# Layer 1's rectifier as one ScalarE function, a 128-row sinks' product, and port ties by deadline, in an attention and two-layer kernel

## The chip, the cores and the metric

One core of one Trainium2 chip runs the whole program. The time is device microseconds (us) of one execution, lower is better. TensorE is called PE, its weight loads PEld, VectorE DVE, ScalarE ACT, GpSimd POOL, SyncE SP.

## The reference, cut to what matters

Attention over a window of 128 keys and the first 4 keys of the sequence (the sinks), then two feed-forward layers without a residual:

```python
B, H, S, D = 2, 8, 768, 64            # n_sink = 4, window = 128
scores = (q @ k.T) / sqrt(D);  keep = (key < 4) or (0 <= query - key < 128)
x = softmax(where(keep, scores, -1e9)) @ v        # -> (1536, 512)
h1 = x @ w1_in;  x = maximum(0.01 * h1, h1) @ w1_out      # d_ff = 2048
h2 = x @ w2_in;  y = (h2 * sigmoid(h2)) @ w2_out
```

## The kernel before, in words

**Tiles.** A unit is one group of 256 queries of one batch and one pair of heads; there are 24, in the order of the groups, and each has two slots of 128 queries. Within a batch the groups are g = 0, 1, 2; the 16 units with g > 0 see the sinks apart from their window. A slot's work: `scores` (PE products `sc`, a DVE reduction that masks them into the tile `P` and keeps the largest in `sm`, the exponential on ACT), `normalise` (a reciprocal in `sm`, and a product by it on ACT for the first 16 slots, on DVE after), `transposes` (PE turns `P` into `tr`, ACT copies that to `pT`). `values` then multiplies `pT` by the values `v` into `at`.

**The sinks.** In a unit with g > 0 the 4 sink columns of both heads go to 24 columns of a tile `psink` in three forms: rounded (hi), the rest (lo), and hi once more. Three small GpSimd operations per slot make them (`normalise`, L619 to L621). PE transposes `psink` into columns of `at`, ACT copies two 32-row strips of it to `sink_t`, and one product `at<-sink_t,sk` of 64 rows (K = 64) and 256 columns begins the sum in `at` (`values`, L660). `sk` holds the sinks' values, made by two DVE operations (`sh`, `sk`) from a loaded tile `sr` (`load_v`).

**The layers.** 16 weight chunks of 128 hidden units per layer. A chunk comes as two halves of raw words (`wr`) and is converted by `load_half`: ACT, four DVE operations on `wb`, ACT and DVE into hi and lo halves of the tile `w` or `we`. Six chunks of layer 1 work beside the attention on tiles of 256 tokens (36 items, `item_h` and `item_y`); after the attention 30 items of layer 1 and 48 of layer 2 work on tiles of 512 tokens. An item is 12 products `h` and 12 products `ya` or `y`, each value as hi and lo parts. Between them `emit_h` makes `ga` (or `gb`), hi and lo, of `h`. In layer 1 that is four steps, of which each waits for the one before: ACT writes 0.01 h to `g`, DVE takes the larger of `g` and `h`, ACT rounds that into hi, DVE subtracts into lo:

```python
R.scalar.activation(g, hp, AF.Copy, scale=0.01)                                    # L474
R.vector.tensor_tensor(g, g, hp, op=ALU.max if layer == 0 else ALU.mult)           # L477
R.scalar.activation(gt[:, 0, :], g, AF.Copy)                                       # L478
R.vector.tensor_tensor(gt[:, 1, :], g, f32(gt[:, 0, :]), op=ALU.subtract)          # L479
```

**What sets the order.** Nothing is issued as it is written. A recorder collects the operations; `deadlines` walks back from TensorE's order to a due time for each; `order` then plays the program with a table of costs and picks, again and again, on each engine the operation that can start first (of equals, the one due first), and of the engines' candidates the one that starts first. A flag `port` marks GpSimd's operations and DVE's with two operands in SBUF (or one in and one out): the plan runs only one of those at a time. The order so found is each engine's queue; the engines then only wait on semaphores. As all instructions are issued from one place, every row of the profile has line L375, and groups go by tiles.

Of the kernel before, what the change touches and what calls it, by code (L numbers as in the profile page):

```python
# [8 lines left out]
F32 = mybir.dt.float32  # L9
F32R = mybir.dt.float32r  # L10
U32 = mybir.dt.uint32
BF16 = mybir.dt.bfloat16
AF = mybir.ActivationFunctionType
ALU = mybir.AluOpType
PSUM = bass.MemoryType.PSUM

P = 128
QB = 128
GT = 256
# [94 lines left out]
class Recorder:  # L114
# [148 lines left out]
    def order(self):  # L263

        for op in self.ops:
            op.need, op.est = len(op.deps), 0.0
            for d in op.deps:
                d.users.append(op)
        self.deadlines()
        free = dict.fromkeys(self.ENGINES, 0.0)  # L270
        dma = port = 0.0
        ready = {e: [o for o in self.ops if o.eng == e and not o.need] for e in self.ENGINES}
        nxt = {(p, t): 0 for p in self.pools for t in p.tiles}
        stages = {}
        for p in self.pools:
            if p.stage is not None:
                stages.setdefault(p.stage, []).append(p)
        n_left = {s: sum(len(ts) for p in ps for ts in p.tiles.values()) for s, ps in stages.items()}
        ended = dict.fromkeys(stages, 0.0)
        done = []  # L280

        def opening(op):

            at = 0.0
            for k, t in enumerate(op.opens):
                p = t.pool
                if nxt[p, t.tag] + sum(o.tag == t.tag for o in op.opens[:k]) != t.place:
                    return None
                if p.stage is not None and p.stage > 0:
                    if n_left[p.stage - 1]:  # L290
                        return None
                    at = max(at, ended[p.stage - 1] + 200)
                k = t.place - p.bufs[t.tag]
                if k >= 0:
                    old = p.tiles[t.tag][k]
                    if old.left:
                        return None
                    at = max(at, old.end + 150)
            return at

        while len(done) < len(self.ops):
            best = None
            for e in self.ENGINES:
                can = []
                for o in ready[e]:
                    at = max(o.est, free[e], port if o.port else 0.0)
                    if o.opens:
                        room = opening(o)
                        if room is None:
                            continue  # L310
                        at = max(at, room)
                    can.append((at, o.due, o.rank, o))
                if not can:
                    continue
                first = min(c[0] for c in can)
                start, _, _, o = min((c for c in can if c[0] <= first), key=lambda c: c[1:3])
                if best is None or start < best[0]:
                    best = (start, o)
            start, op = best
            op.start = start  # L320
            if op.bytes:
                free[op.eng] = start + (500 if op.eng == "sync" else 100)
                dma = max(dma, start + 1200) + max(op.bytes / 350.0, 370)
                end = dma + 300
            else:
                end = free[op.eng] = start + op.cost
                if op.port:
                    port = end
            op.end = end
            ready[op.eng].remove(op)  # L330
            done.append(op)
            for t in op.opens:
                nxt[t.pool, t.tag] += 1
            for t in op.tiles:
                t.left -= 1
                t.end = max(t.end, end)
                if not t.left and t.pool.stage is not None:
                    n_left[t.pool.stage] -= 1
                    ended[t.pool.stage] = max(ended[t.pool.stage], end)
            for u in op.users:  # L340
                u.est = max(u.est, (op.start if not u.deps[op] else end + self.lag(op, u)))
                u.need -= 1
                if not u.need:
                    ready[u.eng].append(u)
        return done
# [44 lines left out]
def attention_moe(ctx, tc, cfg, ins, out):  # L390
    R = Recorder(tc)
    B, H, S, D = cfg["shape"]
    n_sink, window, near = cfg["n_sink"], cfg["window"], cfg["near"]
    qkd, vd, w1, w2 = (ins[n] for n in ("qkd", "vd", "w1", "w2"))
    scale = 1.0 / float(np.sqrt(D))
    NP = H // 2
# [7 lines left out]
    attn = R.pool("attn", 0)  # L404
# [57 lines left out]
    def emit_h(gt, t, layer, T, t0, n):  # L462
        hp = ps.tile([P, 512], F32, "h", 2)[:, :n]
        last = KC * 3 - 1
        i = 0
        with R.group():
            for kc in range(KC):
                for a, b in ((0, xh), (1, xh), (0, xl)):
                    R.tensor.matmul(hp, wi(t, a, kc), b[T][:, kc, t0:t0 + n], start=i == 0, stop=i == last)
                    i += 1  # L470
        R.at_h = R.ops[-1]
        g = keep.tile([P, 512], F32, "g", 2)[:, :n]
        if layer == 0:
            R.scalar.activation(g, hp, AF.Copy, scale=0.01)  # L474
        else:
            R.scalar.activation(g, hp, AF.Sigmoid)
        R.vector.tensor_tensor(g, g, hp, op=ALU.max if layer == 0 else ALU.mult)  # L477
        R.scalar.activation(gt[:, 0, :], g, AF.Copy)  # L478
        R.vector.tensor_tensor(gt[:, 1, :], g, f32(gt[:, 0, :]), op=ALU.subtract)  # L479

    def emit_y(yps, gt, t, layer, c, first, last):
# [8 lines left out]
    if near:  # L490
        mask = [attn.tile([P, 260], BF16, f"mask{i}") for i in range(4)]
        psink = [attn.tile([P, P], F32, f"psink{i}") for i in range(2)]
        sink_t = [attn.tile([64, GT], F32R, f"sink_t{i}") for i in range(2)]

        qk_raw = [attn.tile([P, 2, GT + 388], F32, "qk" if i < 2 else "qkh", 2) for i in range(4)]

# [35 lines left out]
    state, sinks = {}, {}  # L532
# [26 lines left out]
    def load_v(n):  # L559
        if n >= len(units):  # L560
            return
        d = state[n]
        nb = d["nb"]
        d["v"] = attn.tile([P, 3, P], F32, "v", 3)
        R.sync.dma_start(out=d["v"][:, :nb], in_=vd[n][:, :nb])
        key = d["G"] // NG, d["p"]
        if d["g"] > 0 and key not in sinks:
            sr = attn.tile([64, P + 1], F32, "sr", 2)
            R.sync.dma_start(out=sr, in_=ins["vs"][key])

            sh = attn.tile([64, P], F32R, "sh", 1)
            R.vector.tensor_copy(sh, sr[:, :P])
            sinks[key] = attn.tile([64, P], F32R, "sk", NP + 1)
            R.vector.scalar_tensor_tensor(sinks[key], in0=f32(sh), scalar=sr[:, P:P + 1], in1=sr[:, :P],
                                          op0=ALU.mult, op1=ALU.add)

# [26 lines left out]
    def normalise(s):  # L603
        d = slots[s]
        pt, sm, n, i = d["pt"], d["sm"], d["n"], d["i"]
        R.bias = SOONER
        R.vector.tensor_scalar(sm[:, 2:4], sm[:, 2:4], 1.0e-9, None, op0=ALU.add)
        R.vector.reciprocal(sm[:, 2:4], sm[:, 2:4])
        for j in range(2):
            if s < ON_ACT:  # L610
                R.scalar.activation(pt[:, j, :n], pt[:, j, :n], AF.Copy, scale=sm[:, 2 + j:3 + j])
            else:
                R.vector.tensor_scalar(pt[:, j, :n], pt[:, j, :n], sm[:, 2 + j:3 + j], None, op0=ALU.mult)
        if d["g"] > 0:
            s0 = 2 * P if i == 0 else P
            src = pt[:, :, s0:s0 + NS]
            hi, lo, hi2 = (psink[s // 2 % 2][:, o:o + 2 * NS].rearrange("p (j s) -> p j s", j=2)
                           for o in range(32 * i, 32 * i + 6 * NS, 2 * NS))
            R.gpsimd.tensor_copy(hi.bitcast(F32R), src)  # L619
            R.gpsimd.tensor_tensor(lo.bitcast(F32R), src, hi, op=ALU.subtract)  # L620
            R.gpsimd.tensor_copy(hi2, hi)  # L621
        R.bias = 0

    def transposes(s):
# [136 lines left out]
    if near:  # L761
# [7 lines left out]
        for b in range(n_slots + 4):  # L769
            if b == 1:  # L770
                make_mask(2)
                make_mask(3)
                for t in psink:
                    R.gpsimd.memset(t, 0.0)
                for t in sink_t:
                    for k in (0, P):
                        R.vector.tensor_copy(t[:, k:k + P], psink[0][0:64])
            while halves[0] < 2 * NA and b >= W_FIRST + halves[0] * W_EVERY:
                load_half()
            go = b >= OFF and m < (b - OFF + 1) * NA / (2 * NP)  # L780
# [88 lines left out]
def _near_layout(qt, kt, vn, v):  # L869

    B, H, S, D = v.shape
    NP, NG = H // 2, S // GT
    U = B * NG * NP
    qkd = np.zeros((U, P, 2, GT + 388), v.dtype)
    vd = np.zeros((U, P, 3, P), v.dtype)
    vs = np.zeros((B, NP, 64, P + 1), v.dtype)
    for b in range(B):
        for p in range(NP):
            for g in range(NG):
# [71 lines left out]
```

## Time and profile before

| what | us |
|---|---|
| median of 3 runs (lowest, highest) | 642.86 (642.57, 644.47) |
| the profiled execution, its own time | 644.66 |
| its span, first to last instruction | 642.7 |
| PE busy | 623.9 (97%) |
| PEld, DVE, ACT, POOL busy | 525.4, 431.6, 333.3, 58.4 |

The profile is of one execution. Its span is 2.0 us shorter than its own time, and its own time 1.8 us above the median. Busy time of PE overlaps: matmuls are pipelined and their ends are modelled, so what one costs is read from the start of one to the start of the next. "[2.00 <-ACT P L375]" behind a row of a timeline means that the engine had stood idle for 2.00 us and that ACT's writing of `P` ended the wait. PEclk is the clock that TensorE was granted, as a share of 2.4 GHz.

### The profile page before, as it was taken

The page shows a single profiled execution, that of the slowest core. Times are in us where ns is not written, and L with a number is a line of the kernel's source. Part 1 is how long each engine was busy: PE and PEld are TensorE (multiplying, and loading weights), DVE is VectorE, ACT ScalarE, POOL GpSimd, SP SyncE. Part 2 cuts the span into 40 slices and gives each one's busy share as a digit, 9 for nine tenths or more (in the row PEclk, how much of TensorE's full clock was granted, in tenths as well). Part 3 has the DMA queues.
Part 4 walks back from the last instruction along what each step waited for, and adds up shares of the span by engine and source line. Part 5 has one row for each costly group of instructions (what it writes and reads, how often), then busy time and mean ns, then how long its engine had stood idle before and what let it go on. Part 6 is the DMA issues. An engine that isn't in the chain of part 4 may idle for free.

```text
span 642.7 us, 9417 instructions
## 1 busy us (share of the span) xinstructions
PE 623.9 (97%) x3392; PEld 525.4 (82%) x3392; DVE 431.6 (67%) x1033; ACT 333.3 (52%) x738; POOL 58.4 (9%) x137
## 2 busy tenths in 40 slices
PE   7886999999999999999999999999999999999997
PEld 5565899999989888888888887888888888888886
DVE  4898999888748999997424989439733362334254
ACT  6997986888857655453323555346322242222221
POOL 5022433234300000000000000000000000000000
PEclk9997999999999999999999999999999999999999
DMA  8745534533002443333000132203200000000013
GB/s 231 209 156 175 182 109 143 203 108 108 27 2 69 161 155 135 137 132 131 1 0 1 66 132 102 95 1 121 75 0 2 1 1 0 1 1 0 1 65 132
DMA packets 18958, 54.14 MB, mean 84 GB/s; under 512 B 2144, under 2 KB 5984, under 8 KB 18912
## 3 DMA queue, kind: packets, MB, share of 16 engines
q1 hardware_dynamic: 18912, 53.55, 25.1%
q8 instruction: 27, 0.44, 0.3%
q14 instruction: 19, 0.16, 0.1%
HBM read 50.39 MB, written 3.15 MB: 83 GB/s over the span
## 4 chain that ended last, share of the span: by engine, by line
PE 79%; DVE 9%; ACT 7%; DMA 2%; issue 2%; SPq 0%; DVEq 0%; ACTq 0%
PE h L375 35%; PE y L375 31%; PE ya L375 5%; DVE wb L375 4%; PE at L375 4%; ACT P L375 3%; PE sc L375 3%; PE tr L375 2%; DMA wr<-in_w 2%; ACT wb L375 1%; DVE g L375 1%; ACT w L375 1%; DVE P L375 1%; DVE w L375 1%; DVE qkh L375 1%
## 5 line engine op out<-in xcount | busy, mean ns | idle before, releaser
L375 PE MATMUL h<-xh,w 128*128 128x512 f32 (+1 forms) x624 | 161.0, 347 | 0.7 <-DVE w L375 0.4
L375 DVE TENSOR_TENSOR g<-g,h 128x512 f32<-128x512 f32 (+1 forms) x114 | 68.4, 600 | 136.3 <-ACT g L375 136.2
L375 ACT ACTIVATE g<-h 128x512 f32<-128x512 f32 (+1 forms) x114 | 60.1, 527 | 164.2 <-PE h L375 163.6
L375 PEld LDWEIGHTS h<-xh,w 128*128 128x128 f32 x624 | 109.0, 192 | 14.7 <-ACT w L375 0.6
L375 PE MATMUL h<-xl,w 128*128 128x512 f32 (+1 forms) x312 | 106.9, 343 | 0.0
L375 PE MATMUL h<-xh,we 128*128 128x512 f32 x288 | 88.8, 390 | 0.1
L375 DVE SCALAR_TENSOR_TENSOR wb<-wr,wb 128x512 uint32<-128x512 uint32 x128 | 87.7, 698 | 0.4
L375 ACT ACTIVATE gb<-g 128x512 fp32r<-128x512 f32 x78 | 49.3, 632 | 58.0 <-DVE g L375 57.7
L375 DVE TENSOR_TENSOR gb<-g,gb 128x512 fp32r<-128x512 f32 x78 | 53.8, 689 | 26.8 <-ACT gb L375 26.6
L375 PE MATMUL y<-we,gb 128*128 128x512 f32 x288 | 69.5, 390 | 0.1
L375 PE MATMUL y<-w,gb 128*128 128x512 f32 x288 | 68.9, 389 | 0.0
L375 ACT ACTIVATE P<-P,sm 128x260 f32<-128x260 f32 (+2 forms) x128 | 59.7, 486 | 11.6 <-DVE sm L375 10.8
L375 PEld LDWEIGHTS h<-xl,w 128*128 128x128 f32 x312 | 59.8, 192 | 6.6
L375 PEld LDWEIGHTS y<-we,gb 128*128 128x128 f32 x288 | 53.9, 188 | 11.8 <-DVE yp L375 0.6
L375 PEld LDWEIGHTS h<-xh,we 128*128 128x128 f32 x288 | 53.9, 188 | 11.6 <-DVE g L375 0.5
L375 PEld LDWEIGHTS y<-w,gb 128*128 128x128 f32 x288 | 54.1, 188 | 11.2
L375 ACT ACTIVATE wb<-wr 128x512 f32<-128x512 f32 x64 | 42.8, 674 | 36.5 <-DMA wr<-in_w 19.8
L375 PE MATMUL ya<-ga,w 128*128 128x256 f32 x432 | 58.9, 285 | 0.7 <-DVE ga L375 0.6
L375 DVE TENSOR_SCALAR wb<-wb 128x512 uint32<-128x512 uint32 (+1 forms) x128 | 53.7, 430 | 7.6 <-ACT wb L375 6.2
L375 PEld LDWEIGHTS ya<-ga,w 128*128 128x128 f32 x432 | 54.5, 191 | 2.2 <-DVE ga L375 1.0
L375 PE MATMUL h<-xl,we 128*128 128x512 f32 x144 | 56.1, 389 | 0.0
L375 PE MATMUL y<-gb,w 128*128 128x512 f32 x216 | 51.9, 389 | 0.0
(67 smaller groups left out, 768.5 us busy)
## 6 DMA issues: line engine op xcount, KB each, us to landing
wr<-in_w SPq DMA_DIRECT2D x64, 512.0 KB, 3.6
qk<-in_qkd SPq DMA_DIRECT2D x12, 644.0 KB, 3.9
v<-in_vd SPq DMA_DIRECT2D x16, 192.0 KB, 2.7
out_y<-yp SPq DMA_DIRECT2D x11, 256.0 KB, 2.2
qk<-in_qkd SPq DMA_DIRECT2D x4, 512.0 KB, 4.0
v<-in_vd SPq DMA_DIRECT2D x8, 128.0 KB, 3.3
qk<-in_qkd SPq DMA_DIRECT2D x2, 322.0 KB, 7.4
qkh<-in_qkd SPq DMA_DIRECT2D x2, 322.0 KB, 6.5
```

The costliest lines, as they stand in the source:

```text
L375: getattr(eng, name)(*[_real(x) for x in a], **{k: _real(x) for k, x in kw.items()})
```

## The change

Four edits. In layer 1 ACT computes the rectifier itself (`Prelu` with slope 0.01), twice from PSUM: into hi and into `g`; DVE's maximum and ACT's rounding of `g` go, the subtraction stays. `sink_t`, `sh`, `sk` and the loaded `sr` get 128 rows, of which the upper 64 are zero, so that the sinks' product has K = 128. The three small `psink` operations move: hi and the second hi to ACT, lo to DVE. In `order`, of two engines' candidates that start at the same time (as those do that wait for the port), the one due first is taken; before it was the first engine of the list, DVE ahead of GpSimd.

```diff
@@ order
-                if best is None or start < best[0]:
-                    best = (start, o)
-            start, op = best
+                if best is None or (start, o.due) < best[:2]:
+                    best = (start, o.due, o)
+            start, _, op = best
@@ emit_h
         if layer == 0:
-            R.scalar.activation(g, hp, AF.Copy, scale=0.01)
+            R.scalar.activation(gt[:, 0, :], hp, AF.Prelu, alpha=0.01)
+            R.scalar.activation(g, hp, AF.Prelu, alpha=0.01)
         else:
             R.scalar.activation(g, hp, AF.Sigmoid)
-        R.vector.tensor_tensor(g, g, hp, op=ALU.max if layer == 0 else ALU.mult)
-        R.scalar.activation(gt[:, 0, :], g, AF.Copy)
+            R.vector.tensor_tensor(g, g, hp, op=ALU.mult)
+            R.scalar.activation(gt[:, 0, :], g, AF.Copy)
         R.vector.tensor_tensor(gt[:, 1, :], g, f32(gt[:, 0, :]), op=ALU.subtract)
@@ attention_moe, load_v
-        sink_t = [attn.tile([64, GT], F32R, f"sink_t{i}") for i in range(2)]
+        sink_t = [attn.tile([P, GT], F32R, f"sink_t{i}") for i in range(2)]
-            sr = attn.tile([64, P + 1], F32, "sr", 2)
+            sr = attn.tile([P, P + 1], F32, "sr", 2)
-            sh = attn.tile([64, P], F32R, "sh", 1)
+            sh = attn.tile([P, P], F32R, "sh", 1)
-            sinks[key] = attn.tile([64, P], F32R, "sk", NP + 1)
+            sinks[key] = attn.tile([P, P], F32R, "sk", NP + 1)
@@ normalise
-            R.gpsimd.tensor_copy(hi.bitcast(F32R), src)
-            R.gpsimd.tensor_tensor(lo.bitcast(F32R), src, hi, op=ALU.subtract)
-            R.gpsimd.tensor_copy(hi2, hi)
+            R.scalar.activation(hi.bitcast(F32R), src, AF.Copy)
+            R.vector.tensor_tensor(lo.bitcast(F32R), src, hi, op=ALU.subtract)
+            R.scalar.activation(hi2, hi, AF.Copy)
@@ attention_moe
-                        R.vector.tensor_copy(t[:, k:k + P], psink[0][0:64])
+                        R.vector.tensor_copy(t[:, k:k + P], psink[0])
@@ _near_layout
-    vs = np.zeros((B, NP, 64, P + 1), v.dtype)
+    vs = np.zeros((B, NP, P, P + 1), v.dtype)
```

The queues move with it. ACT, before, from the third weight half to the first item's hi part (numbers behind a name count its buffers and allocations):

```order
L375 ACTIVATE wb_2_441<-wr_2_153 128x512
L375 ACTIVATE pT_4_427<-tr_5_433 128x2x256
L375 ACTIVATE P_10_355,sm_10_356<-P_10_355,sm_10_356 128x260 x2
L375 ACTIVATE sink_t0_0_186<-at_2_448 32x128 x2
L375 ACTIVATE w_0_416<-wb_1_401 128x512
L375 ACTIVATE g_0_485<-h_4_451 128x256
L375 ACTIVATE P_11_386,sm_11_387<-P_11_386,sm_11_387 128x260 x2
L375 ACTIVATE P_10_355<-P_10_355,sm_10_356 128x260 x2
L375 ACTIVATE wb_3_499<-wr_3_390 128x512
L375 ACTIVATE w_1_512<-wb_2_441 128x512
L375 ACTIVATE ga_0_518<-g_0_485 128x256
```

The same place of ACT's queue in the changed program:

```order
L375 ACTIVATE wb_2_430<-wr_2_153 128x512
L375 ACTIVATE psink0_0_176<-P_8_295 128x8
L375 ACTIVATE psink0_0_176<-P_9_314 128x8
L375 ACTIVATE psink0_0_176<-psink0_0_176 128x8 x2
L375 ACTIVATE pT_4_416<-tr_5_425 128x2x256
L375 ACTIVATE P_10_355,sm_10_356<-P_10_355,sm_10_356 128x260 x2
L375 ACTIVATE w_0_413<-wb_1_400 128x512
L375 ACTIVATE sink_t0_0_186<-at_2_464 32x128 x2
L375 ACTIVATE ga_0_474<-h_4_440 128x256
L375 ACTIVATE g_0_476<-h_4_440 128x256
```

Four small casts stand ahead of the copy to `pT`, and the two passes over `h` follow each other.

DVE, before, from the third item's lo part (`ga_2`) to the reductions of slot 16 (`P_16`, an ISA row each, followed by the read of its accumulator into `sm`):

```order
L375 TENSOR_TENSOR ga_2_737<-g_2_687,ga_2_737 128x256
L375 TENSOR_SCALAR wb_8_704<-wb_8_704 128x512
L375 CAST sh_2_750<-sr_2_332 64x128
L375 SCALAR_TENSOR_TENSOR wb_8_704<-wr_8_677,wb_8_704 128x512
L375 SCALAR_TENSOR_TENSOR sk_2_759<-sh_2_750,sr_2_332 64x128
L375 SCALAR_TENSOR_TENSOR wb_8_704<-wr_8_677,wb_8_704 128x512
L375 TENSOR_SCALAR sm_14_522<-sm_14_522 128x2
L375 TENSOR_TENSOR w_3_692<-wb_7_668,w_3_692 128x512
L375 RECIPROCAL sm_14_522<-sm_14_522 128x2
L375 TENSOR_TENSOR g_3_739<-g_3_739,h_7_707 128x256
L375 ISA P_16_779,sm_16_780<-sc_32_729,mask2_0_132 128x260
L375 ISA sm_16_780 128x1
```

The same place of DVE's queue in the changed program:

```order
L375 TENSOR_TENSOR ga_2_703<-g_2_705,ga_2_703 128x256
L375 TENSOR_SCALAR wb_8_726<-wb_8_726 128x512
L375 TENSOR_SCALAR sm_14_618<-sm_14_618 128x2
L375 ISA P_16_768,sm_16_769<-sc_32_735,mask2_0_132 128x260
L375 ISA sm_16_769 128x1
L375 SCALAR_TENSOR_TENSOR wb_8_726<-wr_8_654,wb_8_726 128x512
L375 TENSOR_TENSOR w_3_675<-wb_7_641,w_3_675 128x512
L375 SCALAR_TENSOR_TENSOR wb_8_726<-wr_8_654,wb_8_726 128x512
L375 RECIPROCAL sm_14_618<-sm_14_618 128x2
L375 ISA P_16_768,sm_16_769<-sc_33_741,mask2_0_132 128x260
```

`sh_2` and `sk_2` have gone to an earlier place, `g_3` is gone, and the first reduction stands seven rows further ahead.

ACT in the changed program, where layer 2 begins (`g_66` is the first item with a sigmoid); the only other load of a table is the first row of ACT's queue, as before:

```order
L375 ACTIVATE gb_29_4258<-h_69_4228 128x512
L375 ACTIVATE g_65_4261<-h_69_4228 128x512
L375 ACTIVATE wb_48_4267<-wr_48_4244 128x512
L375 ACTIVATE w_15_4292<-wb_46_4217 128x512
L375 ACTIVATE w_15_4292<-wb_47_4250 128x512
L375 ACTIVATE wb_49_4300<-wr_49_4256 128x512
L375 ACT_TABLE_LOAD
L375 ACTIVATE g_66_4307<-h_70_4278 128x512
```

No load of a table stands between the rectifiers and the exponentials.

## Rows read from the trace of the kernel before

**Rows 1.** The page, parts 1 and 2: busy time, PE and granted clock in 40 slices

```profile
PE 623.9 (97%) x3392; PEld 525.4 (82%) x3392; DVE 431.6 (67%) x1033; ACT 333.3 (52%) x738; POOL 58.4 (9%) x137
...
PE   7886999999999999999999999999999999999997
...
PEclk9997999999999999999999999999999999999999
```

**Rows 2.** Windows: busy us of each engine (count), PEclk, DMA share, GB/s

```profile
16.00:32.00 16.00, 13.64 (x82) 8.97 (x81) 13.09 (x55) 15.96 (x52) 1.19 (x6) 1.00 0.72 210
32.00:48.00 16.00, 13.49 (x95) 10.24 (x95) 14.95 (x44) 15.91 (x42) 3.51 (x8) 1.00 0.46 157
48.00:64.00 16.00, 10.93 (x53) 8.57 (x54) 13.74 (x34) 11.72 (x29) 3.83 (x9) 0.73 0.52 175
64.00:80.00 16.00, 14.92 (x114) 13.60 (x113) 15.07 (x45) 15.00 (x39) 6.47 (x11) 0.95 0.51 175
...
224.00:256.00 32.00, 32.00 (x143) 26.48 (x142) 30.89 (x59) 17.10 (x29) 0.00 (x0) 1.00 0.39 134
```

**Rows 3.** Windows around the fall of the clock, columns as in group 2

```profile
52.00:55.50 3.50, 3.50 (x17) 3.50 (x17) 3.44 (x5) 3.49 (x7) 1.59 (x1) 0.51 0.37 95
...
59.00:65.70 6.70, 6.02 (x28) 4.75 (x29) 4.59 (x17) 5.30 (x16) 0.52 (x3) 0.50 0.35 111
```

**Rows 4.** Timeline of PE (start us, us), a unit with the sinks' product

```profile
146.31 0.28 PE L375 MATMUL sc<-qkh 128*128 128x260 f32 x1
146.44 0.28 PE L375 MATMUL sc<-qkh,ql 128*128 128x260 f32 x1
146.65 0.38 PE L375 MATMUL at<-sink_t,sk 64*128 64x256 f32 x1
146.96 1.09 PE L375 MATMUL at<-pT,v 128*64 128x256 f32 x12
```

**Rows 5.** Timeline of PE, a unit without it

```profile
117.08 0.28 PE L375 MATMUL sc<-qkh 128*128 128x256 f32 x1
117.19 0.28 PE L375 MATMUL sc<-qkh,ql 128*128 128x256 f32 x1
117.40 0.87 PE L375 MATMUL at<-pT,v 128*64 128x256 f32 x8
```

**Rows 6.** Groups by shape, 24 to 75 us: the sinks' products there

```profile
L375 PE MATMUL at<-sink_t,sk 64*128 64x256 f32 x4 | 1.7, 430 | 1.3 <-ACT sink_t L375 1.3
```

**Rows 7.** Groups by shape, whole span: count, busy us, mean ns, idle before and releaser

```profile
L375 DVE TENSOR_TENSOR g<-g,h 128x256 f32<-128x256 f32 x36 | 15.0, 415 | 5.0 <-ACT g L375 4.9
...
L375 ACT ACTIVATE ga<-g 128x256 fp32r<-128x256 f32 x36 | 14.7, 409 | 4.4 <-DVE g L375 4.2
L375 ACT ACTIVATE g<-h 128x256 f32<-128x256 f32 x36 | 13.7, 380 | 9.4 <-PE h L375 9.1
```

**Rows 8.** PEld after the attention: its timeline, and the group of `h`

```profile
211.85 0.30 PEld L375 LDWEIGHTS ya<-ga,w 128*128 128x128 f32 x2 [0.24 <-ACT ga L375]
212.34 1.25 PEld L375 LDWEIGHTS ya<-ga,w 128*128 128x128 f32 x10 [0.20 <-DVE ga L375]
...
L375 PEld LDWEIGHTS h<-xh,we 128*128 128x128 f32 x288 | 53.9, 188 | 11.6 <-DVE g L375 0.5
```

**Rows 9.** Groups: ACT's read of an accumulator; DVE's reductions, with their waits

```profile
L375 DVE CUSTOM_DVE_ANT_0 P<-sc,mask 128x260 f32<-128x260 f32 x64 | 25.5, 423 | 7.4 <-PE sc L375 6.3 <-POOL psink L375 0.7
...
L375 ACT ACTIVATION_READ_ACCUMULATOR P<-P,sm 128x1 f32 x96 | 18.5, 192 | 0.0
```

**Rows 10.** Timelines of PE, its two longest pauses

```profile
49.96 0.84 PE L375 MATMUL tr<-ident,P 128*128 128x128 f32 x4 [2.00 <-ACT P L375]
...
59.68 0.59 PE L375 MATMUL sc<-qkh 128*128 128x260 f32 x1 [1.77 <-DVE sm L375]
```

**Rows 11.** Timeline of DVE ahead of the second pause's end; ACT's wait beside it

```profile
56.54 0.21 DVE L375 CAST sh<-sr 64x128 fp32r<-64x128 f32 x1
56.68 0.68 DVE L375 SCALAR_TENSOR_TENSOR wb<-wr,wb 128x512 uint32<-128x512 uint32 x1
57.28 0.34 DVE L375 SCALAR_TENSOR_TENSOR sk<-sh,sr 64x128 fp32r<-64x128 f32 x1
57.54 0.68 DVE L375 SCALAR_TENSOR_TENSOR wb<-wr,wb 128x512 uint32<-128x512 uint32 x1
...
58.89 0.39 DVE L375 TENSOR_TENSOR g<-g,h 128x256 f32<-128x256 f32 x1
59.21 0.41 DVE L375 CUSTOM_DVE_ANT_0 P<-sc,mask 128x260 f32<-128x260 f32 x1
...
58.25 0.63 ACT L375 ACTIVATE w<-wb 128x512 fp32r<-128x512 f32 x1 [2.76 <-DVE wb L375]
```

**Rows 12.** Groups: the loads of ACT's tables

```profile
L375 ACT ACT_TABLE_LOAD x2 | 2.6, 1283 | 0.7 <-PEq L942 0.7
```

## The prediction

> **What bounds the kernel now.** The page first: PE is busy for 97% of the span and nearly full in every slice after the fourth [rows 1]. The windows by stage tell the rest. From 224 us on PE is busy in all of the time, while DVE, the next, has 30.9 of 32 us [rows 2]; there PE's own work is the bound, and neither a shorter DVE operation nor a shorter chain can give anything unless PE waits for it. From 16 to 64 us PE stands idle for 2.4 + 2.5 + 5.1 = 9.9 us, ACT is busy for 15.96 and 15.91 of 16 us, and DVE has 13 to 15 of 16 [rows 2]: a ramp in which ACT bounds first, and the two of them in turn later. So the time has three places to move: PE's own work, a few waits after the attention, and the ramp.
>
> **The sinks' product (K 64 to 128).** PE's work is read from start to start. Two ordinary products follow each other by 0.13 us (146.31 to 146.44); the sinks' product starts 0.21 us after the one ahead of it and the first 64-column product 0.31 us after the sinks' [rows 4], 0.52 us in all. In a unit without sinks the step from a 128-by-128 product to a 64-column one is 0.21 us alone [rows 5]. With 128 rows the sinks' product is of the ordinary kind, so 0.13 + 0.21 = 0.34 us is what I expect from the last score to the first 64-column product, and each unit gains 0.18 us. There are 16; four lie in the ramp, where ACT's `sink_t` ends waits of 1.3 us in front of them [rows 6] and a shorter step hides in the next wait. I count 12: **-2.2 us**; bounds 0 and 16 x 0.18 = -2.9. The upper 64 rows are zeros, set once by copies that exist before too; `sh` and `sk`, 8 of each, get more rows and no more columns; were their steps of 0.14 and 0.26 us [rows 11] to double, DVE would have 3.2 us more over the whole attention, and I count nothing.
>
> One rule speaks against this edit. The Trainium skill, TensorEngine Tiling (Array Packing), section Overview, gives a contraction of 64 or less up to twice the speed when the array is split into row tiles, so that padding to 128 would give speed away; if the present 0.13 us were half of what comes, 12 products would cost 1.6 us more and this term would be about -0.6. The same page, section Tiling Modes, says that a change of the tiling mode drains the engine. The two steps of 0.21 and 0.31 agree with that second sentence, and one product between other shapes has no partner tile to run beside, so I keep the row's value.
>
> **Layer 1's rectifier.** Per item of 256 tokens the chain was ACT 0.38, DVE 0.415, ACT 0.41, then DVE's subtraction [rows 7]. Now ACT reads PSUM twice (2 x 0.38 against 0.38 + 0.41, so ACT's work stays) and DVE loses 0.415. On 66 items that is work beside PE, and PE is full: nothing, but for the waits. After the attention PE's queue waited 0.24 and 0.20 us for `ga` [rows 8], and the chain behind these is a DVE and an ACT step shorter: **-0.4 us**, bounds 0 and -0.9, as `h` waited 0.5 us for DVE's `g` besides [rows 8].
>
> **The casts and the order, in the ramp.** Added on ACT: two casts of 8 columns per slot with sinks, 64 in all, of which 12 stand ahead of the third item's hi part (`ga_2`), by the order. The nearest row is ACT's read of an accumulator, 0.192 us for one column [rows 9]. In the ramp ACT is full, so at most 12 x 0.19 = **+2.3 us**; where ACT waits, nothing, and it does wait: 2.76 us for DVE's `wb` ahead of 58.25 [rows 11]. DVE gets one small subtraction per slot and loses a maximum per item. GpSimd loses 96 operations; DVE waited 0.7 us for one of them [rows 9].
>
> What the ramp gives is read from its two longest pauses. The one that ends at 59.68 waits for `sm` of slot 16 [rows 10], behind a DVE queue that in order holds `wb`, `sh`, `sk`, `wb`, ..., `g`, the reduction. By the order of the changed program `sh` and `sk` have gone ahead and `g` is gone: by starts, 56.54 to 56.68, 57.28 to 57.54 and 58.89 to 59.21, that is 0.14 + 0.26 + 0.32 = 0.7 us [rows 11]. The first reduction is moved seven rows ahead, but the second follows where it was, and TensorE's next score waits for that, so I count 0.7 and no more. The other, 2.00 us for `P` until 49.96 [rows 10], hangs on ACT's queue: there the exponentials of slots 14 and 15 have moved behind, the casts ahead, and I count nothing. With the 0.7 us of DVE's wait for GpSimd the ramp gives **-1.4 us**. Its bounds: +2.3 if every cast delays PE, and on the other side 0.7 + 0.7 + 4.8 = -6.2, where 4.8 is what the granted clock can give back: it fell from 2.4 to 1.2 GHz for 52 to 55.5 and 59 to 65.7 us, after these two pauses, and PE was busy for 3.50 + 6.02 us there [rows 3], half of which is 4.8. I take the value next to the two rows that the order visibly changes, and leave the clock as it was.
>
> **Sum.** -2.2 - 0.4 - 1.4 = -4.0 us. The profiled execution took 644.66 us, 1.8 above the median of the runs, so it would take 640.7; against the median of 642.86 the prediction is 638.9. A measurement of this kernel tells 0.3%, 1.9 us, from no change: faster is under 640.9, slower over 644.8.
>
> **The rivals.**
> - *ACT takes the ramp's gain back* (0.17). For it: ACT is full from 16 to 48 us, and the casts stand right ahead of a copy to `pT` for which PE waits. Against it: its later idle 2.76 us can take them in. Then the ramp gives +2.3 in place of -1.4 and the time is 642.86 - 2.6 + 2.3 = 642.6.
> - *The clock stays low for longer* (0.08), the one that ends slower. The casts lengthen PE's pauses, and the clock, which fell after two pauses of some 2 us, falls once more, for as long as before. Price 4.8 us over the rival above: 647.4. It decides from where PE stands idle for more than the 9.9 us of 16 to 64 us. Against it: by the order the pause at 59.68 gets shorter.
> - *The clock does not fall* (0.12). The pauses break into shorter ones, as the first reduction's new place suggests, and the 4.8 us come back: 638.9 - 4.8 = 634.1, or about 635 if a part of them is hidden behind DVE, which has 15.07 of 16 us from 64 to 80 us [rows 2].
> - *The rectifier needs another table* (0.01), so that the change does not do what it says. If ACT's `Prelu` stood in another table than the exponential, every one of the 36 items beside the attention could bring two loads of 1.28 us [rows 12], 92 us of ACT, which has little idle time until 80 us: some 700 us. The changed program holds two loads, as before, at the same two places. The Trainium skill, ScalarE activation tables: per-element evaluation and per-set limits, section What a function is on this engine, says that two functions in different sets are one load apart and two of one set need none; the trace's 1283 ns agrees with its figure.
>
> **How the numbers follow.** The forecast has 0.62; its own range is 636.5 to 641, by the bounds of the first two terms and a ramp between -3 and 0. Eight in ten reach from the clock's rival, at 634.8, past the 642.6 of the first to 643.0; left out are the slower rival, the tables' and a tail of the clock's. Faster by over 0.3%: nearly all of the forecast, the clock's 0.12 and a little of the first rival, 0.74. Within 0.3%: the rest of the first rival and the upper end of the forecast, 0.18. Slower: 0.08.
>
> **What would show it.** Each step of 0.21 and 0.31 us around the sinks' product becomes 0.13 and 0.21; if not, the first term is wrong. Layer 1's groups show two passes of ACT over `h` of 0.38 us and no maximum, and the waits at 211.85 and 212.34 are gone. DVE's second reduction of slot 16 comes 0.7 us sooner behind `ga_2`, and PE's idle time from 16 to 64 us falls from 9.9 us to about 8.5. More than 11 us there, or a granted clock of 0.5 for over 12 us, makes the prediction wrong; so does a new PE wait after 80 us, as the casts now stand in ACT's queue and wait there for DVE's products, with the copies to `pT` behind them.

## The result, and the profile after

| | median us (lowest, highest), runs |
|---|---|
| before | 642.89 (642.57, 644.47), 4 |
| after | 638.24 (637.16, 638.79), 4 |

The ratio after to before is 0.9908 with a 95% interval of 0.9887 to 0.9928: faster by 4.6 to 7.3 us; the two medians lie 4.65 us apart, at the near end of that. The prediction was 638.9. The profiled execution of after took 638.0 us, span 636.0; that of before 644.66. The four executions of after had mean granted clocks of 1.0 (638.0 and 637.16 us) and 0.995 (638.47 and 638.79). The page of after, parts 1 and 2:

```profile
PE 616.7 (97%) x3392; PEld 521.4 (82%) x3392; DVE 406.3 (64%) x999; ACT 335.5 (53%) x802; POOL 32.9 (5%) x41
...
PE   7877899999999999999999999999999999999997
...
PEclk9999999999999999999999999999999999999999
```

Against [rows 1] PE is busy for 7.2 us less (part of it because nothing runs at the low clock), DVE for 25.3 us less, ACT for 2.2 us more, and the granted clock has no fall in it. The windows of after, columns as in [rows 2]:

```profile
16.00:32.00 16.00, 12.97 (x78) 8.35 (x77) 12.96 (x52) 16.00 (x53) 0.00 (x0) 1.00 0.85 227
32.00:48.00 16.00, 12.73 (x91) 10.08 (x92) 15.61 (x50) 15.86 (x46) 0.16 (x1) 1.00 0.54 175
48.00:64.00 16.00, 12.26 (x90) 9.94 (x89) 15.41 (x44) 15.05 (x44) 2.67 (x2) 1.00 0.52 172
64.00:80.00 16.00, 14.36 (x116) 12.83 (x116) 15.16 (x42) 14.81 (x44) 2.86 (x2) 1.00 0.56 184
80.00:96.00 16.00, 15.92 (x140) 14.27 (x137) 14.40 (x68) 14.64 (x53) 2.64 (x2) 1.00 0.35 110
224.00:256.00 32.00, 32.00 (x143) 26.50 (x142) 29.10 (x55) 15.91 (x28) 0.00 (x0) 1.00 0.49 167
```

From 16 to 64 us PE idles for 3.03 + 3.27 + 3.74 = 10.0 us, as much as before (9.9), and from 64 to 80 us 1.6 against 1.1. After 80 us it is full, as it was.

Where the time went is read by putting the same product of the two traces side by side. The first `h` product of the 12th item (of the 36 beside the attention) starts at 101.14 us before and at 97.96 after: the ramp ends 3.2 us sooner. From there to the 36th item the lead grows to 5.6 us, in steps of 0.19 to 0.20 at nine units with sinks and one of 0.68 at 118 to 119 us, where before PE waited for `sm`. Behind the attention it grows by 0.6, and at the change of layers by 0.5, to 6.7. The last 0.5 is not the change's: four kernels that leave that stage as it was (before with 128 rows, with the casts, with the new rule for ties, with the pauses filled) gain 0.48 there too, so it belongs to before's profiled execution.

The timeline of PE after, a unit with the sinks' product, shows those steps:

```profile
142.07 0.28 PE L375 MATMUL sc<-qkh 128*128 128x260 f32 x1
142.19 0.28 PE L375 MATMUL sc<-qkh,ql 128*128 128x260 f32 x1
142.31 0.28 PE L375 MATMUL at<-sink_t,sk 128*128 128x256 f32 x1
142.52 1.09 PE L375 MATMUL at<-pT,v 128*64 128x256 f32 x12
```

The two steps are 0.12 and 0.21 us, where [rows 4] have 0.21 and 0.31. The groups that the change made (count, busy us, mean ns, idle before and its releaser):

```profile
L375 ACT ACTIVATE ga<-h 128x256 fp32r<-128x256 f32 x36 | 13.7, 381 | 8.4 <-PE h L375 8.2
L375 ACT ACTIVATE g<-h 128x256 f32<-128x256 f32 x36 | 13.7, 381 | 0.5 <-DVE ga L375 0.3
L375 ACT ACTIVATE psink<-P 128x8 fp32r<-128x8 f32 x32 | 6.2, 208 | 1.4 <-DVE P L375 1.3
L375 ACT ACTIVATE psink<-psink 128x8 f32<-128x8 f32 x32 | 6.2, 204 | 0.4
L375 DVE TENSOR_TENSOR psink<-P,psink 128x8 fp32r<-128x8 f32 x32 | 5.9, 194 | 2.4 <-ACT psink L375 2.2
L375 ACT ACT_TABLE_LOAD x2 | 2.6, 1283 | 0.8 <-PEq L943 0.7
```

The second pass of ACT over `h` hardly waits (0.5 us in 36), the maximum of [rows 7] is gone, the table loads are the two of [rows 12]. PE's pauses in the ramp, from its timeline after, with what ended them:

```profile
28.81 0.84 PE L375 MATMUL tr<-ident,P 128*128 128x128 f32 x4 [1.22 <-ACT P L375]
...
40.99 0.30 PE L375 MATMUL at<-ident,psink 128*128 128x128 f32 x1 [0.86 <-DVE psink L375]
...
42.83 0.39 PE L375 MATMUL at<-sink_t,sk 128*128 128x256 f32 x1 [1.54 <-ACT sink_t L375]
...
50.18 0.84 PE L375 MATMUL tr<-ident,P 128*128 128x128 f32 x4 [1.00 <-ACT P L375]
...
58.25 0.39 PE L375 MATMUL sc<-qkh 128*128 128x260 f32 x1 [0.94 <-DVE sm L375]
...
66.44 0.38 PE L375 MATMUL h<-xh,w 128*128 128x256 f32 x1 [1.17 <-ACT w L375]
```

The two pauses of 2.00 and 1.77 us [rows 10] have become a string of pauses of 1.54 us at most, and the clock stayed at 2.4 GHz in this execution. The casts bring a wait of their own, 0.86 us at 40.99. The `sc` product at 58.25 now follows DVE's second reduction of slot 16. From DVE's timelines, the third item's lo part and that reduction, first before, then after:

```profile
55.87 0.41 DVE L375 TENSOR_TENSOR ga<-g,ga 128x256 fp32r<-128x256 f32 x1
...
59.55 0.42 DVE L375 CUSTOM_DVE_ANT_0 P<-sc,mask 128x260 f32<-128x260 f32 x1
```

```profile
54.81 0.42 DVE L375 TENSOR_TENSOR ga<-g,ga 128x256 fp32r<-128x256 f32 x1
...
57.78 0.41 DVE L375 CUSTOM_DVE_ANT_0 P<-sc,mask 128x260 f32<-128x260 f32 x1
```

The distance is 3.68 us before and 2.97 after, shorter by the 0.7 us that the prediction read from the order.

### The profile page after: what moved, and what is told of

It is laid out like the page before. It is cut to its first block, busy times and chain, and to the rows that moved or that the text cites. A ratio compares the mean times of both kernels' runs of the same rounds, so it can differ in the third digit from the quotient of the medians.

```text
span 636.0 us, 9261 instructions
## 1 busy us (share of the span) xinstructions
PE 616.7 (97%) x3392; PEld 521.4 (82%) x3392; DVE 406.3 (64%) x999; ACT 335.5 (53%) x802; POOL 32.9 (5%) x41
## 4 chain that ended last, share of the span: by engine, by line
PE 85%; ACT 9%; DMA 2%; DVE 2%; issue 1%; SPq 0%; DVEq 0%; ACTq 0%
PE h L375 39%; PE y L375 33%; PE ya L375 5%; ACT P L375 4%; PE sc L375 3%; PE at L375 3%; PE tr L375 2%; DMA wr<-in_w 2%; ACT wb L375 1%; ACT w L375 1%; DVE wb L375 1%; ACT pT L375 1%; ACT qkh L375 1%; DMA qk<-in_qkd 0%; ACT ga L375 0%
## 5 line engine op out<-in xcount | busy, mean ns | idle before, releaser
L375 PE MATMUL h<-xh,w 128*128 128x512 f32 (+1 forms) x624 | 159.2, 344 | 1.6 <-ACT w L375 1.2
L375 PEld LDWEIGHTS h<-xh,w 128*128 128x128 f32 x624 | 107.6, 189 | 15.4 <-ACT w L375 1.4
L375 DVE TENSOR_TENSOR g<-g,h 128x512 f32<-128x512 f32 x48 | 32.9, 685 | 107.8 <-ACT g L375 107.8
L375 DVE TENSOR_SCALAR wb<-wb 128x512 f32<-128x512 f32 (+1 forms) x128 | 54.4, 430 | 7.5 <-ACT wb L375 5.7
L375 ACT ACTIVATE gb<-g 128x512 fp32r<-128x512 f32 x48 | 30.3, 632 | 34.4 <-DVE g L375 34.0
```

The source lines that it names most:

```text
L375: getattr(eng, name)(*[_real(x) for x in a], **{k: _real(x) for k, x in kw.items()})
```

## The experiments

Ratios are to runs of before on the same chip; the last column is how much later (+) or earlier than in before's trace the 12th item's first `h` product starts. That column is of one execution each and has some noise of its own: after and the kernel with the old rule for ties have the same queues up to 98 us and differ by 0.5. Before itself had medians of 642.9, 643.92 and 644.3 us over 15, 20 and 26 runs.

| kernel | median us | ratio, 95% interval | 12th item, us |
|---|---|---|---|
| after | 638.24 | 0.9908 (0.9887, 0.9928) | -3.2 |
| after, sinks' product with 64 rows | 640.84 | 0.9951 (0.9930, 0.9971) | -3.7 |
| after, old rectifier | 644.4 | 1.0020 (1.0000, 1.0039) | +1.6 |
| after, casts on GpSimd | 636.09 | 0.9878 (0.9854, 0.9903) | -5.0 |
| after, old rule for ties | 638.96 | 0.9920 (0.9896, 0.9944) | -3.7 |
| before, 128 rows | 642.15 | 0.9973 (0.9958, 0.9989) | -1.5 |
| before, new rectifier | 651.54 | 1.0116 (1.0094, 1.0137) | +8.9 |
| before, casts on ACT and DVE | 647.53 | 1.0050 (1.0030, 1.0069) | +2.2 |
| before, new rule for ties | 645.16 | 1.0024 (1.0005, 1.0042) | +0.1 |
| before, new rectifier and 128 rows | 648.0 | 1.0075 (1.0049, 1.0101) | +7.0 |
| before, new rectifier in before's order | 641.01 | 0.9959 (0.9944, 0.9973) | -2.4 |
| casts exchanged in the order made without them | 641.68 | 0.9969 (0.9952, 0.9987) | +1.9 |
| before, PE's two pauses filled | 645.2 | 1.0019 (1.0006, 1.0033) | +0.1 |

**One part of the change undone.** *The sinks' product with 64 rows:*

```diff
-sink_t = [attn.tile([P, GT], F32R, ...
+sink_t = [attn.tile([64, GT], F32R, ...       # sr, sh, sk and the zeroing likewise
```

> The changed kernel with the sinks' product of 64 rows again; the order of every engine is the changed one. Theory (each 64-row product costs 0.18 us of steps before and behind it): the steps around it are 0.21 and 0.31 us again, 12 to 16 of them cost 2.2 to 2.9 us, time 640.3 to 641.2. Rival (a row tile of 64 costs nothing, or is faster; the gain comes from the order): 638 or less.

640.84 us: 2.6 slower than after. In its trace the lead over before stands still from 115 us to the 36th item, at 4.36 us, where after's grows by 0.19 to 0.20 per unit. The time lies in the range expected: the term holds. One thing more shows in this trace, as its queues are those of after: the granted clock was at 1.2 GHz for 6.8 us (43.7 to 47.1 and 60.8 to 64.2), and the 12th item still starts 0.5 us sooner than in after's, where it never was. Windows up to that item, columns as in [rows 2], first after, then this kernel (one execution of each, here the fastest of six):

```profile
0.00:97.96 97.96, 82.40 (x575) 66.52 (x576) 82.51 (x300) 89.05 (x274) 17.40 (x32) 1.00 0.62 184
```

```profile
0.00:97.45 97.45, 84.49 (x576) 69.05 (x576) 81.64 (x300) 88.84 (x274) 17.21 (x32) 0.96 0.62 182
```

PE is busy for 2.1 us more and idle for 2.6 us less.

*The old rectifier:*

```diff
-R.scalar.activation(gt[:, 0, :], hp, AF.Prelu, alpha=0.01)
-R.scalar.activation(g, hp, AF.Prelu, alpha=0.01)
+R.scalar.activation(g, hp, AF.Copy, scale=0.01)
+R.vector.tensor_tensor(g, g, hp, op=ALU.max)
+R.scalar.activation(gt[:, 0, :], g, AF.Copy)
```

> The changed kernel with layer 1's rectifier in four steps again (ACT, DVE's maximum, ACT, DVE). Theory (the shorter chain removes a few waits at 118, 212, 219 and 386 us, 1.8 us in all, and gives a little in the ramp): 639.5 to 642, with those waits back and DVE busier by 30 us. Rival (PE is full, DVE's time is worth nothing): 638.2 +- 0.5.

644.4 us, above what the theory and its rival expected: beside the other parts the rectifier, with the order that the planner writes for it, is worth 6.2 us, and without it the change is no gain. From 16 to 96 us PE waits for `ga` here, at the end of the longer chain, 2.8 us for DVE's half and 1.2 for ACT's, where after has no such wait:

```profile
PE ya L375 <- DVE ga L375: 2.8, 3, 1.2
```

*The casts back on GpSimd:*

```diff
-R.scalar.activation(hi.bitcast(F32R), src, AF.Copy)
-R.vector.tensor_tensor(lo.bitcast(F32R), src, hi, op=ALU.subtract)
-R.scalar.activation(hi2, hi, AF.Copy)
+R.gpsimd.tensor_copy(hi.bitcast(F32R), src)
+R.gpsimd.tensor_tensor(lo.bitcast(F32R), src, hi, op=ALU.subtract)
+R.gpsimd.tensor_copy(hi2, hi)
```

> The changed kernel with the three psink operations on GpSimd again. Theory (the casts cost in the ramp: PE waits there 0.86 us for DVE's psink and 1.54 us for sink_t, and ACT is full): these waits shrink, 636 to 638. Rival (GpSimd's hold on the shared port cost more than that): 639 to 641.

636.09 us (635.83 to 637.5): the fastest kernel of all, 2.15 us under after by the medians, though the intervals of the two ratios overlap. The theory's 636 to 638 holds. PE's waits from 16 to 96 us (in all, times, longest), first after, then this kernel (the longest):

```profile
PE tr L375 <- ACT P L375: 4.0, 5, 1.2
PE sc L375 <- DVE sm L375: 2.5, 4, 0.9
PE at L375 <- ACT sink_t L375: 1.8, 2, 1.5
```

```profile
PE at L375 <- ACT sink_t L375: 2.6, 3, 1.4
PE at L375 <- ACT w L375: 1.4, 1, 1.4
PE sc L375 <- DVE sm L375: 1.4, 3, 0.8
...
PE tr L375 <- ACT P L375: 0.6, 2, 0.4
```

With the casts in its queue ACT is later with `P`: 4.0 us of waits against 0.6. As the two orders differ too (before, with its casts on GpSimd, has 3.1), this does not show that it is the casts; the last run below, which keeps the order, does.

*The old rule for ties* (the three lines of `order` as before):

> The changed kernel with the planner's old rule for ties. Its queues differ in some 20 rows of DVE and 4 of ACT, all after 90 us, where PE does not wait; PE's queue is the same. Theory: the same time, 638.2 +- 0.6. Rival (the rule removes waits at 118 us): 639 or more, with a wait of some 0.5 us for sm near 115 us.

638.96 us, between the theory's 638.8 and the rival's 639: beside the casts, the rule is worth 0.7 us or nothing.

**One part alone.** *128 rows:*

```diff
-sink_t = [attn.tile([64, GT], F32R, ...
+sink_t = [attn.tile([P, GT], F32R, ...       # sr, sh, sk and the zeroing likewise
```

> The kernel before with the sinks' product of 128 rows and nothing else; the order of every engine is that of before. Theory: steps of 0.13 and 0.21 us around the product, 2.2 to 2.9 us less than before, 640.0 to 640.7. Rival (nothing, as the gain lies in the order): 642.9.

642.15 us, ratio 0.9973, which is 1.7 us (0.7 to 2.7), less than the 2.2 to 2.9 expected, though the interval reaches them; the queues are those of before. From the 12th item to the 36th the lead grows from 1.5 to 3.3 us, 9 units of 0.19 to 0.20. The 1.5 in the ramp cannot be put down to the edit, as the execution had a mean granted clock of 0.997 against 0.992 in before's trace.

*The new rectifier:*

```diff
-R.scalar.activation(g, hp, AF.Copy, scale=0.01)
+R.scalar.activation(gt[:, 0, :], hp, AF.Prelu, alpha=0.01)
+R.scalar.activation(g, hp, AF.Prelu, alpha=0.01)
-R.vector.tensor_tensor(g, g, hp, op=ALU.max)
-R.scalar.activation(gt[:, 0, :], g, AF.Copy)
```

> The kernel before with the Prelu rectifier and nothing else. Theory (waits after 100 us go, 1.8 us; the ramp moves by the new order, -2 to +1): 639 to 642. Rival (nothing, PE is full): 642.9 +- 0.6. No added load of a table, ACT's second load still ahead of layer 2.

651.54 us, 7.6 slower than before: both times expected were missed, while the loads of tables stayed two, as expected. At the 12th item the trace is 8.9 us late, afterwards it gains. Its windows in the ramp (columns as in [rows 2]):

```profile
60.00:64.00 4.00, 1.25 (x9) 0.81 (x8) 3.63 (x9) 3.16 (x9) 3.44 (x6) 0.89 0.06 25
64.00:68.00 4.00, 3.22 (x13) 2.92 (x14) 3.94 (x10) 0.55 (x2) 0.77 (x1) 0.50 0.81 269
68.00:72.00 4.00, 3.84 (x25) 3.64 (x24) 3.61 (x9) 2.78 (x6) 0.00 (x0) 0.76 0.44 140
72.00:76.00 4.00, 0.41 (x3) 0.21 (x3) 3.97 (x10) 1.52 (x4) 0.00 (x0) 1.00 0.40 118
```

and the same stretch of the kernel with the casts on GpSimd:

```profile
60.00:64.00 4.00, 3.85 (x27) 3.22 (x27) 3.97 (x11) 4.00 (x13) 1.08 (x4) 1.00 0.20 78
64.00:68.00 4.00, 3.01 (x22) 2.73 (x22) 3.97 (x15) 3.96 (x12) 0.89 (x3) 1.00 0.54 168
68.00:72.00 4.00, 4.00 (x37) 3.55 (x38) 3.79 (x15) 3.44 (x8) 2.22 (x3) 1.00 0.89 272
72.00:76.00 4.00, 4.00 (x35) 3.89 (x34) 2.51 (x4) 3.83 (x11) 3.47 (x6) 1.00 0.45 139
```

In the slow kernel DVE is full, while ACT works for 0.55 and 1.52 of 4 us and PE, in the last window, for 0.41. What DVE does there, and what PE then waits for, from the timelines:

```profile
74.26 0.42 DVE L375 TENSOR_SCALAR wb<-wb 128x512 uint32<-128x512 uint32 x1
74.71 0.69 DVE L375 SCALAR_TENSOR_TENSOR wb<-wr,wb 128x512 uint32<-128x512 uint32 x1
75.32 0.42 DVE L375 CUSTOM_DVE_ANT_0 P<-sc,mask 128x260 f32<-128x260 f32 x1
```

```profile
75.81 0.39 PE L375 MATMUL sc<-qkh 128*128 128x260 f32 x1 [3.58 <-DVE sm L375]
```

Conversions of weights (`wb`) stand ahead of the reduction that PE needs. That is a matter of the queue, and three runs below put it to the test. The granted clock is at 1.2 GHz in this ramp too, for 20.5 us in all up to 87 us against 10.2 in before's trace.

*The casts:* the three lines of the diff above, exchanged in before.

> The kernel before with the psink operations on ACT and DVE and nothing else. Theory (ACT is full from 16 to 48 us, casts of 0.1 to 0.2 us each in its queue): 0 to 2.3 us more than before, 642.9 to 645.2. Rival (GpSimd's port was the cost): 641 to 642.5.

647.53 us, ratio 1.0050: slower by 3.2 us (1.9 to 4.4), more than the 2.3 expected at most. So moving the casts costs time alone and in company; alone, PE's order moved with them from 27.6 us on.

*PE's two pauses filled* with 14 and 10 products that nobody reads, added to TensorE's work ahead of the pauses of [rows 10]:

```diff
+for op, t, a, b, n in self.fill:
+    for _ in range(n):
+        op.calls.append(("matmul", (t[:, 256:512], a, b), dict(start=True, stop=True)))
...
```

> The kernel before with 14 and 10 products added that nobody reads, in PE's two pauses ahead of 49.96 and 59.68 us, written to an unused half of h. Theory (the clock's fall after these pauses costs up to 4.8 us of ramp): the granted clock stays 1.00 from 48 to 80 us and the time is 638.5 to 641. Rival (DVE and ACT bound the ramp, a slow PE hides behind them): the clock stays up and the time is 642.9 +- 0.6. Third: the clock falls all the same, and the time is 642.9 or more.

645.2 us: no gain, as in the third outcome expected, though the clock fell for less long than before. Its windows over the two falls of [rows 3]:

```profile
52.00:55.50 3.50, 2.70 (x16) 2.10 (x16) 3.44 (x6) 3.50 (x8) 2.09 (x4) 1.00 0.52 147
55.50:59.00 3.50, 2.37 (x11) 2.17 (x12) 3.50 (x8) 0.83 (x3) 0.96 (x1) 0.76 0.82 297
59.00:65.70 6.70, 6.30 (x49) 5.31 (x49) 5.25 (x21) 5.86 (x16) 0.53 (x3) 0.87 0.41 127
```

The clock stood at 1.00 and 0.87 where it had 0.51 and 0.50, and the 12th item came no sooner; a shorter fall came in between, at 57.3 to 60.7 us. As the 24 products take PE's time too (0.12 us each, 2.9 in all), this alone doesn't price the clock.

**Order or operation.** *The new rectifier with 128 rows, without casts and tie rule.* Queues of PE, ACT and GpSimd are those of the rectifier alone; the fastest kernel is this one with the tie rule added:

```diff
-if best is None or (start, o.due) < best[:2]:
-    best = (start, o.due, o)
-start, _, op = best
+if best is None or start < best[0]:
+    best = (start, o)
+start, op = best
```

> Before with the rectifier and the 128 rows, without the casts and the tie rule. TensorE's, ScalarE's and GpSimd's queues are word for word those of the rectifier alone (651.5 us); the kernel with the tie rule added as well is the one that measured 636.1. If the parts act through the order that the planner writes for the ramp: 649 us (647.5 to 650.5), 651.5 less the 2.6 of the sinks' products, the whole surplus over before reached by 100 us, and the one line on ties worth some 13 us here, though it was worth nothing beside the casts. If each part has a price of its own that adds up, ties nothing: 636 to 640 us.

648.0 us, as expected if the parts act through the order, against 636.09 with the rule: 12 us for a rule that moved 0.7 us in after, and all of it is there at the 12th item (+7.0 against -5.0). The clock, at 1.2 GHz for 17.1 us of this ramp and 3.4 of the other, is not the main cause: one execution of this kernel had a mean granted clock of 0.995 and took 646.24 us, two of the other had 0.995 and took 636.09 and 636.1. The same wait for `sm` is there:

```profile
75.89 0.59 PE L375 MATMUL sc<-qkh 128*128 128x260 f32 x1 [3.42 <-DVE sm L375]
```

*The tie rule alone in before* (the same three lines the other way):

> Before with the tie rule alone. If ties have a price of their own, it was at most 0.7 us beside the other parts: 642.2 to 643.6 us. If they act through the ramp's order, which here differs from both kernels' in TensorE's, VectorE's and ScalarE's queues, the time can lie some us to either side (636 to 650), and the start of the layer-0 products after 100 us is moved by that same amount.

645.16 us, ratio 1.0024: another order, 0.1 to 0.4% slower. The rule has no price of its own.

*The new rectifier in before's order.* The planner is given the old operations; when it has written the order, they are exchanged, the maximum for an ACT pass at its place:

```diff
+for (a, b, c), g, gt, hp in self.swap:
+    a.calls = [("activation", (g, hp, AF.Prelu), dict(alpha=0.01))]
+    b.calls = [("activation", (gt, hp, AF.Prelu), dict(alpha=0.01))]
+    b.eng, c.calls = "scalar", []
...
```

> Before with the rectifier's operations exchanged after the planner has written the order of before: TensorE's, GpSimd's and SyncE's queues are word for word those of before; each maximum on VectorE becomes a ScalarE pass at its place, and the old ScalarE copy is gone. If the rectifier alone was slow through its order: 641.0 to 643.0 us (0 to 1.9 below before: the waits for g after 210 us gone, VectorE lighter in the ramp). If ScalarE's load by the two passes from PSUM made it slow: 645 to 651 us.

641.01 us, ratio 0.9959, at the low end of what was expected if the order made the rectifier slow: the operation itself gives 1.7 to 3.6 us, and the order that the planner writes for it in before takes 10 us away (651.54 against 641.01). PE's wait for DVE's `sm` from 16 to 96 us, first before, then this kernel:

```profile
PE sc L375 <- DVE sm L375: 4.0, 6, 1.8
```

```profile
PE sc L381 <- DVE sm L381: 2.8, 5, 1.1
```

*The casts in the order made without them* (after's operations in the queues of the 636.09 us kernel, the three casts exchanged at their places):

```diff
+for (a, b, c), hi, hi2, src in self.swap:
+    a.calls = [("activation", (hi.bitcast(F32R), src, AF.Copy), {})]
+    c.calls = [("activation", (hi2, hi, AF.Copy), {})]
+    a.eng, b.eng, c.eng = "scalar", "vector", "scalar"
...
```

> The changed kernel's operations, casts included, in the order that the planner writes for the kernel with the casts on GpSimd (636.1 us): TensorE's and SyncE's queues are word for word those of that kernel; the casts are exchanged for ScalarE and VectorE operations at their places afterwards. If the casts' 2.1 us came from the order: 635.3 to 636.9 us. If they came from the casts' own time on ScalarE and VectorE: 637.5 to 639 us.

641.68 us: both theories missed. The casts cost 5.6 us at their old places (5 us in its five executions with a mean granted clock of 0.999 or more) and 2.15 where the planner puts them, so here the operations cost and the order wins some of it back. From 16 to 96 us PE waits 2.1 us for `P` and 1.6 for `psink`, with the same queue of PE in which it waited 0.6 and 0.5. Two of the pauses in its timeline:

```profile
41.39 0.30 PE L380 MATMUL at<-ident,psink 128*128 128x128 f32 x1 [1.04 <-ACT psink L380]
...
67.91 0.84 PE L380 MATMUL tr<-ident,P 128*128 128x128 f32 x4 [1.28 <-ACT P L380]
```

## Why the prediction was right, and where not

The time and its side were right; the sum came about in another way than written, and that it came within 0.7 us of the median is in part luck: a gain of the rectifier and a loss by the casts, both larger than written, offset each other in the ramp. Two of its figures are not what they are said to be worked out from: the bounds of the terms add up to 636.1 to 642.9, wider than its range of 636.5 to 641, and 634.8 is neither of the two times, 634.1 and 635, that the clock's rival was given.

- **The sinks' product, -2.2:** right in size and mechanism. The steps are those expected to 0.01 us, a unit gains 0.19 to 0.20, and the edit measured 2.6 us in company, 1.7 alone. The rule of the Trainium skill that was weighed against it (TensorEngine Tiling (Array Packing), section Overview) brings nothing for this lone product: from the score ahead of it to the first 64-column product PE takes 0.33 us with 128 rows (142.19 to 142.52) and 0.52 with 64 [rows 4]. Both steps around it are shorter, by 0.09 and 0.10 us, which agrees with the sentence on draining in the same page of the Trainium skill, section Tiling Modes.
- **The rectifier, -0.4:** mis-sized. The step that failed is "PE is full: nothing, but for the waits", taken for all 66 items. It holds behind the attention, where the lead grows by 0.6 us in 30 items; of its two waits [rows 8] the one for ACT is gone, and one of 0.26 us for DVE's `ga` stays. It fails ahead of 80 us, where PE waits and DVE, with seven maxima of 0.41 us, is nearly as full as ACT. In before's order this term measured 2.6 us; PE's waits for `sm` fall from 4.0 to 2.8 us, and those of 0.6 us for DVE's `ga` go. Its trace is 2.4 us ahead at the 12th item, and some of that may be the clock's, which was at 1.2 GHz for 6.8 us against before's 10.2; but among executions with a mean clock of 0.997 it still takes about 2 us less than before (640.16 to 640.92 against 642.25 to 643.54).
- **The ramp, -1.4:** the trace is 3.2 us ahead at the 12th item, in part by other causes than the two counted. The one read from the order came: DVE's second reduction follows 0.7 us sooner behind `ga_2`, and the pause at 59.68 shrank (1.77 to 0.94 us, with the `sc` product starting at 58.25). But "0.7 us of DVE's wait for GpSimd", a gain, belongs to an edit that costs 2 to 3 us, near the bound of +2.3 that was kept for the range: a cast takes 0.208 us, close to the 0.192 of the row that it was priced by. So the rival "ACT takes the ramp's gain back" was near the truth for the casts (PE waits longer for ACT's `P` and for `psink` in the order made without them); the rectifier's larger gain hid it. PE's idle time, expected to fall from 9.9 to 8.5 us, stayed at 10.0.
- **The clock.** That it would not fall was a rival at 0.12; it did not in two of the four executions. Its 4.8 us look too many, and what a fall costs stays open. The 4.8 counted all of PE's busy time at 1.2 GHz as lost, though a part of it can lie ahead of a wait for DVE or ACT that ends no sooner. Of 61 runs of before, the 20 with a mean granted clock of 0.996 or more (0.997 at most) have a median of 642.66 us, the 25 with 0.993 or less 644.84: a longer fall goes with 2.2 us. In after, 0.995 against 1.0 goes with 1 us. Neither tells cause from effect. Against a fixed price stands the kernel with 64 rows, whose queues are those of after: its clock was at 1.2 GHz for 6.8 us of the ramp, and what PE was busy longer it waited less. The gain of the whole change does not hang on the clock: the two executions of after with 0.995 still lie 4.0 us below those 20 of before. The two traces are 6.7 us apart and the medians 4.65, as before's profiled execution was 1.8 us above its median and after's 0.2 below.
- **The order.** Its price was read at two places of two queues. The runs show that the ramp's order as a whole moves the time by 10 to 12 us with the same or nearly the same operations, more than any operation of the change, and that a part's price depends on the others: undone one by one, they give 2.6, 6.2, -2.15 and 0.7 us, 7.3 in all against 4.65 measured. The range covered the outcome, but no rival named this. Which of the planner's ties turns the order at 60 us stays open.

## What to carry to other kernels

Where a planner writes the queues, an edit is two edits, the operation and the order that the planner makes of its cost; keep the old order once, exchange the operations in it, and the two can be priced apart. Read a price in the stage where the engine is full: a maximum whose going gave 0.6 us over 30 items beside a full PE was worth some 2 us more where DVE fed an idle one. And an operation that is taken from an idle, slow engine and given to a full one can cost more than it saves, however short it is.

## What was not expected of the hardware

A lone product of 64 rows among products of 128 costs 0.19 to 0.20 us more than the same product padded with 64 rows of zeros. ACT's cast of 8 columns takes 0.20 us, more than half of the 0.38 us of its pass over 256 columns. And the granted clock fell to 1.2 GHz in the kernel with the casts on GpSimd too (its mean was 0.79 from 40 to 44 us and 0.78 from 44 to 48), which is the fastest of all: a fall of the clock in the ramp is no measure of the whole.
